# A linear-attention and Fourier-mix kernel on one core: keys and queries transposed on TensorE, 64-row score products, the bonus term through TensorE, and loads in a fixed order

## The chip, the core and the metric

The kernel runs on one core of a Trainium2 chip. A core has five engines, each with its own instruction queue that runs in order: TensorE (PE in the profile; its weight loads are shown apart as PEld), VectorE (DVE), ScalarE (ACT), GpSimd (POOL) and SyncE (SP), which here only issues transfers. Sixteen DMA engines move the data. Matrix products land in PSUM, eight banks of 2 KB for each of 128 partitions; all other tiles lie in SBUF.

The metric is device time in microseconds for one execution. Kernels are compared by the median of their runs.

## The reference

Two stages. The first is a recurrent linear attention: for each batch and head a state of 48 by 48 decays by `w` at each of 768 steps and takes up an outer product; the current step's own product enters the output with the weight `u` in place of the decay. The second adds the real part of a Fourier transform over sequence and model width, normalizes, and runs an MLP of two products with a residual.

```python
# B, H, S, D = 4, 8, 768, 48
for t in range(S):
    cur = np.einsum('bhd,bhe->bhde', u[None] * kt, vt)
    y[:, :, t] = np.einsum('bhd,bhde->bhe', rt, state + cur)
    state = w[None, :, :, None] * state + np.einsum('bhd,bhe->bhde', kt, vt)
...
mixed = np.real(np.fft.fft(np.fft.fft(x, axis=1), axis=2))
u = x + mixed                      # d_model = 384
un = (u - mean(u)) / np.sqrt(var(u) + 1e-06)
out = u + np.maximum(un @ w_ch1, 0.0) @ w_ch2      # 384 -> 1536 -> 384
```

## The kernel before

**Attention.** Each batch (4) is cut into 6 chunks of 128 steps, and each chunk holds all 8 heads. Keys are scaled by a falling power of the decay (`wpn`, L172) and queries by a rising one (`wpp`, L176), both into one bfloat16 tile `KR` of 12 blocks of 128 columns: four blocks with the keys of two heads each (pairs, heads at columns 0 and 64), and eight with the queries of one head each, the other half zero. A DMA transpose (L181) turns the whole tile into `KRT`. Four products (L195) give the scores of the chunk in two PSUM tiles `A_ps`, one with the first four heads, one with the last four; the strictly upper part is kept, for one tile on DVE (L200), for the other by a copy on ACT (L204) and a select on POOL (L205). `y_ps` sums the part of the state (L211, eight products) and the values under the masked scores (L214, eight products). The state is carried by `u_ps` (L219, L222) and scaled by DVE into `Sst` (L224). The bonus term is made apart: POOL multiplies `rt` by `kt` and by `u` (L183, L184), DVE sums over the head (L186), POOL spreads it over the values (L188, `TT`). DVE adds it to `y_ps` (L226): that is `X` of the chunk.

**Fold, Fourier, MLP.** Sums and differences of the two halves of the sequence and of the width (`fold`, L236 to L240) feed the Fourier stage: products with tables (L251), copies by ACT (L253), a reversal by DVE (L256), products with the second tables (L270 to L274), the residual (L276), statistics and normalization (L279 to L289) and a DMA transpose into `UNT` (L291). The MLP of a batch is 2 x (36 + 36) products of 384 columns, L301 and L307, with the ReLU on ACT (L303), the residual on DVE (L310) and the store (L312).

**Order.** The framework puts the instructions of each engine in an order at build time. Attention and Fourier stages have a higher priority than the MLP, and among the former the order of the program counts: attention of batch b+1, then Fourier of b, then the MLP of b-1. All loads, both kinds of DMA transpose, the tables and the stores are issued on SP's queue, where the framework chose their order too; POOL's queue issues the weights. PSUM holds two banks for `A_ps`, one each for `y_ps` and `u_ps`, and four for `mm`, the tile of the Fourier stage and the MLP. Load buffers (`inp`) are five deep, `KR` three, `KRT` three.

Of the kernel before, what the change touches and what calls it, by code (L numbers as in the profile page):

```python
# [62 lines left out]
def kernel(  # L63
# [13 lines left out]
    inp = ctx.enter_context(tc.tile_pool(name="inp", bufs=5))  # L77
# [12 lines left out]
    wall = cp.tile([128, DM + NP], F32, name="wall")  # L90
    nc.vector.memset(wall[:, DM:], 1.0)
    nc.sync.dma_start(out=wall[:, 0:DM], in_=w.rearrange("h d -> (h d)").partition_broadcast(128))
    wv = w.rearrange("(p a) d -> a d p", a=2)
    nc.gpsimd.dma_start(out=wall[0:D, DM:], in_=wv[0])
    nc.gpsimd.dma_start(out=wall[64:64 + D, DM:], in_=wv[1])
# [6 lines left out]
    nc.vector.tensor_scalar(out=ncol, in0=icol, scalar1=-1.0, scalar2=1.0, op0=AluOp.mult, op1=AluOp.subtract)  # L102
    eps_t = cp.tile([128, 1], F32, name="eps_t")
    nc.vector.memset(eps_t, 1e-6)

    lw = cp.tile([128, DM + NP], F32, name="lw")
    nc.scalar.activation(lw, wall, Act.Ln)
    wpp = cp.tile([128, H, D], F32, name="wpp")
    wpn = cp.tile([128, H, D], F32, name="wpn")
    lwr = lw[:, 0:DM].rearrange("p (h d) -> p h d", h=H)  # L110
    nc.scalar.activation(wpn, lwr, Act.Exp, scale=ncol[:, 0:1])  # L111
    nc.scalar.activation(wpp, lwr, Act.Exp, scale=icol[:, 0:1])
    wdec = cp.tile([128, NP], F32, name="wdec")
    nc.scalar.activation(wdec, lw[:, DM:], Act.Exp, scale=float(L))
    WD = cp.tile([128, NP, 2, D], F32, name="WD")
    urow = cp.tile([128, H, D], F32, name="urow")
    ident = cp.tile([128, 128], BF16, name="ident")
    mtri = cp.tile([128, 128], BF16, name="mtri")
# [8 lines left out]
    nc.gpsimd.memset(WD, 0.0)  # L127
    for a in range(2):
        rows = slice(a * 64, a * 64 + 64)
        nc.vector.tensor_copy(WD[rows, :, a, :], wdec[rows, :].unsqueeze(2).to_broadcast([64, NP, D]))  # L130

# [7 lines left out]
    def load_tables():  # L139
        nc.sync.dma_start(out=te_t, in_=te_c.ap())  # L140
        nc.sync.dma_start(out=to_t, in_=to_c.ap())
        nc.sync.dma_start(out=hid_t, in_=hid_c.ap())
        for dt in range(3):
            nc.gpsimd.dma_start(out=W1[:, dt, :], in_=w1[dt * 128:(dt + 1) * 128, :])
        for fg in range(3):
            nc.gpsimd.dma_start(out=W2[:, fg * 4:(fg + 1) * 4, :],
                                in_=w2[fg * 512:(fg + 1) * 512, :].rearrange("(f p) d -> p f d", p=128))

    count = [0]

    def attention(b):
# [4 lines left out]
        for q in range(NQ):  # L156
            i = count[0]
            count[0] += 1
            sl = slice(q * 128, (q + 1) * 128)
            rt = inp.tile([128, H, D], F32, name="rt")  # L160
            kt = inp.tile([128, H, D], F32, name="kt")
            vt = inp.tile([128, H, D], F32, name="vt")
            nc.sync.dma_start(out=kt, in_=k[b, :, sl, :].rearrange("h p d -> p h d"))
            nc.sync.dma_start(out=rt, in_=r[b, :, sl, :].rearrange("h p d -> p h d"))
            nc.sync.dma_start(out=vt, in_=v[b, :, sl, :].rearrange("h p d -> p h d"))
            if i == 0:
                nc.sync.dma_start(out=urow, in_=u.partition_broadcast(128))
                nc.sync.dma_start(out=mtri, in_=mtri_c.ap())
                nc.sync.dma_start(out=ident, in_=id_c.ap())
            KR = KRs[i % NB]  # L170
            K = KR[:, 0:4, :]
            nc.vector.tensor_tensor(out=K.rearrange("t p (a d) -> t p a d", a=2)[:, :, :, 0:D],  # L172
                                    in0=kt.rearrange("t (p a) d -> t p a d", a=2),
                                    in1=wpn.rearrange("t (p a) d -> t p a d", a=2), op=AluOp.mult)
            for a in range(2):
                nc.vector.tensor_tensor(out=KR[:, 4 + a:12:2, a * 64:a * 64 + D], in0=rt[:, a::2, :],  # L176
                                        in1=wpp[:, a::2, :], op=AluOp.mult)
            V = wp.tile([128, H, D], BF16, name="V")
            nc.scalar.copy(V, vt)  # L179
            KRT = wp.tile([128, 12, 128], BF16, name="KRT")  # L180
            nc.sync.dma_start_transpose(out=KRT, in_=KR.rearrange("t c d -> t (c d)"))  # L181
            T1 = wp.tile([128, H, D], F32, name="T1", bufs=2)
            nc.gpsimd.tensor_tensor(out=T1, in0=rt, in1=kt, op=AluOp.mult)  # L183
# [3 lines left out]
            TT = wp.tile([128, H, D], BF16, name="TT")  # L187
            nc.gpsimd.tensor_tensor(out=TT, in0=V, in1=DE.unsqueeze(2).to_broadcast([128, H, D]), op=AluOp.mult)  # L188

# [166 lines left out]
```

## Time and profile before

| | us |
|---|---|
| median of 3 runs | 293.69 (292.69 to 295.96) |
| the profiled execution | 292.54 |
| its span in the trace | 290.8 |
| DMA transposes `KRT`, issue to landing | 24 of 4.1 (median) |
| loads k, r, v, issue to landing | 72 of 3.6 to 3.7 (median) |
| `te_t` needed / landed | PE waited 9.3 |

In the profile's groups a row gives line, engine, operation, tiles with partitions by elements, count, busy us in all, mean ns of one, and the idle time ahead of it with what ended it. Busy time of PE counts a product from its start to its modelled end, and products overlap in the array; so what a stream of products costs is read from the distance between starts, not from the mean of one. A group with more than one shape has a mean of them all.

### The profile page before, as it was taken

How to read it: one execution, taken by the hardware profiler on the slowest of the kernel's cores; microseconds unless marked ns; L12 is line 12 of the kernel's file. 1: busy time of each engine (PE TensorE's matmuls, PEld its weight loads, DVE VectorE, ACT ScalarE, POOL GpSimd, SP SyncE). 2: the span in 40 equal slices, each digit the busy share in tenths (PEclk: the TensorE clock that was granted, in tenths of full speed). 3: DMA queues.
4: the chain of work that ended last, by engine and by line, in shares of the span. 5: the costliest groups of instructions: out<-in, count | busy, mean ns of one | idle time of the engine just before them, and what ended most of it. 6: DMA issues, size and time to landing. Idle time of an engine off the chain costs nothing. (4 is left out here: it accounts for less than half of the span.)

```text
span 290.8 us, 3776 instructions
## 1 busy us (share of the span) xinstructions
PE 178.5 (61%) x1336; PEld 110.2 (38%) x1336; DVE 152.2 (52%) x318; ACT 105.5 (36%) x208; POOL 97.5 (34%) x113
## 2 busy tenths in 40 slices
PE   0034123011643264098654697999699996999995
PEld 0023112001432142055532364656355564666662
DVE  0494459816977589339799885519210290201202
ACT  2701110020221122046232396742928429256170
POOL 8665452978488725002766522000000000000000
PEclk9999999999999999999955799999899999999999
DMA  6899999999988999910962409310501104201102
GB/s 141 169 193 179 200 196 187 188 218 211 193 172 160 175 199 205 246 62 0 189 111 54 95 12 206 98 55 0 112 27 54 57 0 108 83 11 70 56 27 81
DMA packets 128546, 34.91 MB, mean 120 GB/s; under 512 B 122896, under 2 KB 127760, under 8 KB 128528
## 3 DMA queue, kind: packets, MB, share of 16 engines
q1 hardware_dynamic: 126448, 32.32, 53.8%
q0 software_dynamic: 2080, 2.36, 5.4%
q8 instruction: 10, 0.16, 0.2%
q14 instruction: 8, 0.07, 0.1%
HBM read 20.52 MB, written 4.72 MB: 87 GB/s over the span
## 5 line engine op out<-in xcount | busy, mean ns | idle before, releaser
L303 ACT ACTIVATE HT<-mm 128x384 bf16<-128x384 f32 x96 | 44.9, 489 | 28.4 <-PE mm L301 28.3
L301 PE MATMUL mm<-UNT,W 128*128 128x384 bf16 x288 | 51.9, 337 | 4.9 <-ACT HT L303 4.6
L307 PE MATMUL mm<-W,HT 128*128 128x384 bf16 x288 | 50.0, 326 | 0.0
L310 DVE TENSOR_TENSOR osb<-mm,UF 128x384 f32<-128x384 f32 x24 | 13.3, 555 | 68.6 <-PE mm L307 68.4
L195 PE MATMUL A_ps<-KRT 128*128 128x256 bf16 x96 | 22.7, 381 | 30.9 <-DMA KRT<-KR 28.6
L301 PEld LDWEIGHTS <-W 128*128 128x128 bf16 x288 | 28.7, 100 | 25.5 <-issue 8.3
L204 ACT CAST AC<-A_ps 128x512 bf16<-128x512 f32 x24 | 14.0, 585 | 60.4 <-PE A_ps L195 60.4
L307 PEld LDWEIGHTS <-HT 128*128 128x128 bf16 x288 | 27.8, 98 | 17.5
L188 POOL TENSOR_TENSOR TT<-V,DE 128x384 bf16<-128x384 bf16 x24 | 20.0, 836 | 42.8 <-DVE X L226 26.2
L219 PE MATMUL u_ps<-V,KR 128*128 128x96 bf16 x80 | 9.5, 257 | 39.7 <-ACT V L179 18.4
L183 POOL TENSOR_TENSOR T<-rt,kt 128x384 f32<-128x384 f32 x24 | 25.9, 1078 | 12.3 <-DMA rt<-in_r_dram 9.4
L179 ACT CAST V<-vt 128x384 bf16<-128x384 f32 x24 | 12.3, 512 | 47.5 <-DMA vt<-in_v_dram 26.0
L176 DVE TENSOR_TENSOR KR<-rt,wpp 128x192 bf16<-128x192 f32 x48 | 26.0, 573 | 3.5 <-DMA rt<-in_r_dram 3.2
L172 DVE TENSOR_TENSOR KR<-kt,wpn 128x384 bf16<-128x384 f32 x24 | 18.7, 784 | 15.6 <-ACT wpn L111 9.8
L184 POOL TENSOR_TENSOR T<-T,urow 128x384 f32<-128x384 f32 x24 | 26.4, 1104 | 1.3
L205 POOL TENSOR_SCALAR_AFFINE_SELECT MA<-AC 128x512 bf16<-128x512 bf16 x24 | 16.8, 702 | 26.0 <-ACT AC L204 21.1
L195 PEld LDWEIGHTS <-KRT 128*128 128x128 bf16 x96 | 10.4, 125 | 38.3 <-DMA KRT<-KR 33.8
L219 PEld LDWEIGHTS <-KR 128*128 128x128 bf16 x80 | 6.6, 121 | 43.0 <-issue 17.8
L214 PE MATMUL y_ps<-V,MA 128*128 128x48 bf16 x192 | 12.4, 205 | 15.6 <-DVE MA L200 9.2
L253 ACT CAST TT<-mm 128x386 bf16<-128x386 f32 (+1 forms) x24 | 12.4, 594 | 22.5 <-PE mm L251 22.5
L200 DVE TENSOR_TENSOR MA<-A_ps,mtri 128x512 bf16<-128x512 f32 x24 | 16.4, 682 | 7.6 <-PE A_ps L195 6.3
L186 DVE TENSOR_REDUCE DE<-T 128x8 f32<-128x384 f32 x24 | 13.1, 545 | 12.0 <-POOL TT L188 10.2
(58 smaller groups left out, 228.4 us busy)
## 6 DMA issues: line engine op xcount, KB each, us to landing
kt<-in_k_dram SPq DMA_DIRECT2D x24, 192.0 KB, 3.6
rt<-in_r_dram SPq DMA_DIRECT2D x24, 192.0 KB, 3.6
vt<-in_v_dram SPq DMA_DIRECT2D x24, 192.0 KB, 3.7
out_dram<-osb SPq DMA_DIRECT2D x24, 192.0 KB, 1.9
W<-in_moe_w_ch_dram POOLq DMA_DIRECT2D x6, 384.0 KB, 7.0
hid_t<-hid_c SPq DMA_DIRECT2D x1, 576.0 KB, 5.2
KRT<-KR SPq DMA_TRANSPOSE x24, 4.1
te_t<-te_c SPq DMA_DIRECT2D x1, 289.5 KB, 4.5
```

The lines of the kernel that those rows point to most:

```text
L172: nc.vector.tensor_tensor(out=K.rearrange("t p (a d) -> t p a d", a=2)[:, :, :, 0:D], in0=kt.rearrange("t (p a) d -> t p a d", a=2), in1=w ...
L176: nc.vector.tensor_tensor(out=KR[:, 4 + a:12:2, a * 64:a * 64 + D], in0=rt[:, a::2, :], in1=wpp[:, a::2, :], op=AluOp.mult)
L183: nc.gpsimd.tensor_tensor(out=T1, in0=rt, in1=kt, op=AluOp.mult)
L184: nc.gpsimd.tensor_tensor(out=T1, in0=T1, in1=urow, op=AluOp.mult)
L188: nc.gpsimd.tensor_tensor(out=TT, in0=V, in1=DE.unsqueeze(2).to_broadcast([128, H, D]), op=AluOp.mult)
L195: nc.tensor.matmul(A_ps[:, 2 * pp:2 * pp + 2, :], lhsT=KRT[:, p, :], rhs=KRT[:, 4 + 2 * p:6 + 2 * p, :], start=(pp == 0), stop=(pp == 1), ...
L200: nc.vector.tensor_tensor(out=MA, in0=A_ps, in1=mtri.unsqueeze(1).to_broadcast([128, 4, 128]), op=AluOp.mult)
L205: nc.gpsimd.affine_select(out=MA, in_=AC, pattern=[[0, 4], [1, 128]], base=0, channel_multiplier=-1, compare_op=AluOp.is_gt, fill=0.0)
L219: nc.tensor.matmul(u_ps[:, p, :, :], lhsT=KR[:, p, :], rhs=V[:, 2 * p:2 * p + 2, :], start=(p == 0), stop=(q == 0 and p == NP - 1), skip_g ...
L301: nc.tensor.matmul(hp, lhsT=W1[:, dt, ft * 128:(ft + 1) * 128], rhs=UNT[:, :, dt, :], start=(dt == 0), stop=(dt == 2))
L303: nc.scalar.activation(out=HT[:, ft, :], in_=hp, func=Act.Relu)
L307: nc.tensor.matmul(op, lhsT=HT[:, ft, j * 128:(j + 1) * 128], rhs=W2[:, ft, :], start=(ft == 0), stop=(ft == 11))
```

## The change

- Keys and queries are loaded into one tile `kr` and scaled by one DVE product (L191) with one table `wtab`; `KR` has 2 x 4 blocks, keys and queries both as pairs of heads, with no half zero.
- The DMA transpose goes. PE transposes the eight blocks through the identity into one PSUM bank `tp` (L202), and ACT copies it to `KRT` (L204).
- The scores are eight products of 128 columns that use 64 rows each (one head, L212): even heads in one `A_ps`, odd heads in the other. The state's part is four products of 96 columns (L233) where there were eight of 48.
- The bonus: DVE multiplies transposed keys by transposed queries (`PR`, L206), four products of 2 columns with the weights `UW` (L229) sum it into eight further columns of the output's PSUM tile (`yd_ps`), ACT copies them (`DE`, L236). Two POOL products and DVE's reduction go.
- One bank moves from `mm` (four to three) to `tp`. `MA` has six buffers, `inp` six. DVE clears `KR` and `WD` in place of POOL.
- Loads: all of a batch are issued in program order on SP (`keep_in_program_order`), batch 0's first, then the tables, then batch 1's; batch b+2's behind the `UNT` transposes of b. Weights are issued by POOL after the third chunk's `TT`. Stores move from SP to POOL.
- Fourier of b now stands ahead of attention of b+1 in the program.
- ACT loads its function tables at two fixed places at the start.

```diff
-    inp = ctx.enter_context(tc.tile_pool(name="inp", bufs=5))
+    inp = ctx.enter_context(tc.tile_pool(name="inp", bufs=6))
...
+    nc.scalar.preload_act_table_set("natural_log_exp_and_others")
...
+    tc.keep_in_program_order(nc.scalar.preload_act_table_set("sqrt_and_others"))
...
-        t = cp.tile([128, 12, 128], BF16, name=f"KR{i}")
-        nc.gpsimd.memset(t, 0.0)
+        t = cp.tile([128, 2, NP, 128], BF16, name=f"KR{i}")
+        nc.vector.memset(t, 0.0)
...
+    def load_weights():
+        with tc.issue_after(marks["tt2"].ins):
+            for dt in range(3):
+                nc.gpsimd.dma_start(out=W1[:, dt, :], in_=w1[dt * 128:(dt + 1) * 128, :])
...
+    def loads(b):
+        ins = []
+        for q in range(NQ):
...
+            sp(nc.sync.dma_start(out=kr[:, 0], in_=k[b, :, sl, :].rearrange("h p d -> p h d")))
+            sp(nc.sync.dma_start(out=kr[:, 1], in_=r[b, :, sl, :].rearrange("h p d -> p h d")))
...
-            KRT = wp.tile([128, 12, 128], BF16, name="KRT")
-            nc.sync.dma_start_transpose(out=KRT, in_=KR.rearrange("t c d -> t (c d)"))
-            T1 = wp.tile([128, H, D], F32, name="T1", bufs=2)
-            nc.gpsimd.tensor_tensor(out=T1, in0=rt, in1=kt, op=AluOp.mult)
-            nc.gpsimd.tensor_tensor(out=T1, in0=T1, in1=urow, op=AluOp.mult)
-            DE = wp.tile([128, H], F32, name="DE")
-            nc.vector.reduce_sum(out=DE, in_=T1, axis=AX.X)
...
+            tp = ps.tile([128, 2, NP, 128], BF16, name="tp", bufs=1)
+            for s in range(2):
+                for p in range(NP):
+                    nc.tensor.transpose(tp[:, s, p, :], KR[:, s, p, :], ident)
+            KRT = wp.tile([128, 2, NP, 128], BF16, name="KRT")
+            nc.scalar.copy(KRT, tp)
+            PR = wp.tile([128, NP, 128], BF16, name="PR")
+            nc.vector.tensor_tensor(out=PR, in0=KRT[:, 0], in1=KRT[:, 1], op=AluOp.mult)
...
+                for a in range(2):
+                    rows = slice(a * 64, a * 64 + 64)
+                    nc.tensor.matmul(A_ps[a][:, p, :], lhsT=KRT[rows, 0, p, :], rhs=KRT[rows, 1, p, :],
+                                     start=(p == 0), stop=(p == NP - 1), skip_group_check=True)
...
+            for p in range(NP):
+                nc.tensor.matmul(yd_ps[:, DM + 2 * p:DM + 2 * p + 2], lhsT=PR[:, p, :], rhs=UW[:, p, :],
+                                 start=(p == 0), stop=False, skip_group_check=True)
...
+                for p in range(NP):
+                    nc.tensor.matmul(y_ps[:, 2 * p:2 * p + 2, :], lhsT=KRT[:, 1, p, :], rhs=Sst[:, p, :, :],
+                                     start=False, stop=False, skip_group_check=True)
+            DE = wp.tile([128, H], F32, name="DE")
+            nc.scalar.copy(DE, yd_ps[:, DM:])
...
-                fp = ps.tile([128, 2, m], F32, name="mm", bufs=4)
+                fp = ps.tile([128, 2, m], F32, name="mm", bufs=3)
...
-            nc.sync.dma_start(out=out[b, row:row + 128, :], in_=osb)
+            nc.gpsimd.dma_start(out=out[b, row:row + 128, :], in_=osb)
...
+    ins = loads(0)
     load_tables()
-    xs = [attention(0)]
+    xs = [attention(0, ins)]
+    load_weights()
+    ins = loads(1)
...
-            if b + 1 < B:
-                xs.append(attention(b + 1))
             if b < B:
                 hs.append(fourier(b, *xs[b]))
+            if b + 1 < B:
+                xs.append(attention(b + 1, ins))
+            if b + 2 < B:
+                ins = loads(b + 2)
```

What this does to the order on three engines follows; a number behind a tile's name tells one buffer in time from another.

SP's queue before, in the loads of batch 1 (`kt`, `rt`, `vt`), with transposes of earlier chunks among them:

```order
L163 DMA kt_985<-in_k_dram 128x8x48
L164 DMA rt_984<-in_r_dram 128x8x48
L163 DMA kt_1043<-in_k_dram 128x8x48
L165 DMA vt_986<-in_v_dram 128x8x48
L164 DMA rt_1042<-in_r_dram 128x8x48
L181 DMA_TRANSPOSE KRT_588<-KR2_99 128x12x128
L165 DMA vt_1044<-in_v_dram 128x8x48
```

SP's queue after, from the last loads of batch 1 to the first of batch 2 (`kr` takes keys and queries):

```order
L171 DMA kr_559<-in_k_dram 128x8x48
L172 DMA kr_559<-in_r_dram 128x8x48
L175 DMA vt_560<-in_v_dram 128x8x48
L320 DMA_TRANSPOSE UNT_600<-UN_640 128x9x128
L320 DMA_TRANSPOSE UNT_646<-UN_686 128x9x128
L171 DMA kr_1057<-in_k_dram 128x8x48
L172 DMA kr_1057<-in_r_dram 128x8x48
```

The transposes of a chunk are gone from the queue, and the only ones left, those of a batch's normalized rows, stand between two batches' loads.

DVE's queue before, in batch 0 (`T1` is the bonus before its sum):

```order
L224 TENSOR_TENSOR Sst_335<-u_ps_329,WD_91 128x384
L172 TENSOR_TENSOR KR1_97<-kt_343,wpn_86 128x8x48
L186 TENSOR_REDUCE DE_296<-T1_293 128x8
L176 TENSOR_TENSOR KR1_97<-rt_342,wpp_85 128x4x48 x2
L186 TENSOR_REDUCE DE_358<-T1_355 128x8
L200 TENSOR_TENSOR MA_303<-A_ps_300,mtri_94 128x512
L226 TENSOR_TENSOR X_109<-y_ps_312,TT_298 128x384
```

DVE's queue after, in batch 1 on the way to batch 2, whose first product `KR0_102` is already there:

```order
L255 TENSOR_TENSOR X_691<-yd_ps_907,TT_918 128x384
L191 TENSOR_TENSOR KR0_102<-kr_1057,wtab_92 128x16x48
L206 TENSOR_TENSOR PR_951<-KRT_949 128x512
L218 TENSOR_TENSOR MA_963<-A_ps_953,mtri_74 128x512
L253 TENSOR_TENSOR Sst_1271<-u_ps_1266,WD_100 128x384
L206 TENSOR_TENSOR PR_1013<-KRT_1011 128x512
L255 TENSOR_TENSOR X_691<-yd_ps_969,TT_980 128x384
```

Three scaling products and a reduction became one scaling product and `PR`; chunks overlap in the order, here with `PR` of one chunk ahead of `X` of the one before.

ACT's queue before, in batch 0:

```order
L204 CAST AC_193<-A_ps_189 128x512
L204 CAST AC_251<-A_ps_247 128x512
L179 CAST V_289<-vt_282 128x384
L204 CAST AC_309<-A_ps_305 128x512
L179 CAST V_351<-vt_344 128x384
```

ACT's queue after, at the same place:

```order
L204 COPY KRT_350<-tp_341 128x1024
L222 CAST AC_367<-A_ps_355 128x512
L196 CAST V_405<-vt_142 128x384
L204 COPY KRT_416<-tp_407 128x1024
L236 COPY DE_379<-yd_ps_370 128x8
L222 CAST AC_433<-A_ps_421 128x512
```

The copy of the transposed tile of the next chunk (`KRT_416`) now stands ahead of the bonus copy of this one (`DE_379`) on the same engine. On PE the order sets, in many chunks, one score product of the next chunk ahead of the eight products of this chunk's masked scores with the values, and the other seven behind. The MLP of batch 0 stands behind Fourier 1: 61 of its products ahead of batch 3's first transposes, most others among batch 3's chunks, and the last few inside Fourier 2.

More of the change, by code (lines that the diff above doesn't have):

```diff
@@ L206, in attention @@
                                             channel_multiplier=-1, compare_op=AluOp.is_gt, fill=0.0)
                 MAs.append(MA)
[L208 to L215 removed]
+            yd_ps = ps.tile([128, DM + H], F32, name="yd_ps", bufs=1)
@@ L304, in mlp @@
         for j in range(3):
-            op = ps.tile([128, DM], F32, name="mm", bufs=4)
+            op = ps.tile([128, DM], F32, name="mm", bufs=3)
             for ft in range(12):
```

151 lines of the change are left out of this document (76 added, 75 removed).

## The prediction

> **What bounds the kernel now.** I read the page first: the span, the busy shares and the forty slices, in which one digit is a tenth of a slice of 7.3 us.
>
> ```profile
> span 290.8 us, 3776 instructions
> PE 178.5 (61%) x1336; PEld 110.2 (38%) x1336; DVE 152.2 (52%) x318; ACT 105.5 (36%) x208; POOL 97.5 (34%) x113
> ...
> PE   0034123011643264098654697999699996999995
> ...
> DMA  6899999999988999910962409310501104201102
> ```
>
> There are two halves. Up to about 125 us the DMA engines are full and PE is nearly idle; from about 180 us PE is full and the DMA engines are not. Next I asked for single lines (minimum, median and maximum in ns, then first and last start) to find the border between the halves.
>
> ```profile
> L226 DVE TENSOR_TENSOR X<-y_ps,TT x24: 527/554/559, 23.0 to 181.6; 128x384 bf16<-128x384 f32 x24
> L301 PE MATMUL mm<-UNT,W x288: 322/326/524, 165.3 to 281.2; 128*128 128x384 bf16 x144
> ```
>
> X (L226) ends a chunk of the attention. The first ends at 23.5 us, the last at 182.2, and the MLP (L301) starts only at 165.3, since it follows the attention of later batches in the order. So the time is that of the last X plus a tail. The tail by stage, with busy us and count for PE, PEld, DVE, ACT and POOL, then clock, DMA share and GB/s; the last row is a dense piece of the attention:
>
> ```profile
> 182.20:203.70 21.50, 21.46 (x143) 13.28 (x142) 11.44 (x30) 10.03 (x21) 0.00 (x0) 1.00 0.18 51
> 203.70:238.70 35.00, 32.70 (x201) 19.32 (x199) 11.06 (x33) 18.27 (x39) 0.00 (x0) 0.95 0.19 52
> 238.70:290.80 52.10, 46.34 (x283) 27.46 (x281) 8.15 (x18) 25.60 (x55) 0.00 (x0) 0.99 0.20 61
> 135.70:163.60 27.90, 15.85 (x174) 10.50 (x174) 24.62 (x48) 9.02 (x17) 18.47 (x20) 0.76 0.64 109
> ```
>
> The first three rows end with the last transforms of batch 2, of batch 3, and the program. Before 182 us the list of waits (total us, times, longest) names the cause:
>
> ```profile
> PEld L195 <- DMA KRT<-KR: 33.8, 16, 7.0
> PE mm L251 <- DMA te_t<-te_c: 9.3, 1, 9.3
> ...
> SPq L181 <- DVE KR L176: 29.5, 9, 9.5
> ```
>
> PE waits for the DMA transposes, and the queue that issues them (SPq L181) itself stands still for 29.5 us until DVE has made their input, with loads queued behind. The Fourier stage even waits for its tables.
>
> **The change, part by part.** I price a chunk of 128 steps on each engine, then the path.
>
> ```profile
> L172 DVE TENSOR_TENSOR KR<-kt,wpn x24: 541/674/1342, 11.2 to 173.8; 128x384 bf16<-128x384 f32 x24
> L172 DVE TENSOR_TENSOR KR<-kt,wpn 128x384 bf16<-128x384 f32 x24 | 18.7, 784 | 15.6 <-ACT wpn L111 9.8 <-DMA KRT<-KR 4.6 <-DMA kt<-in_k_dram 0.9
> L176 DVE TENSOR_TENSOR KR<-rt,wpp x48: 343/351/1664, 13.5 to 175.0; 128x192 bf16<-128x192 f32 x48
> L236 DVE TENSOR_TENSOR EO<-X x6: 348/554/1546, 45.0 to 182.5; 128x384 bf16<-128x384 bf16 x3, 128x1152 bf16<-128x1152 bf16 x3
> 182.50 0.75 DVE L236 TENSOR_TENSOR EO<-X 128x1152 bf16<-128x1152 bf16 x1
> L200 DVE TENSOR_TENSOR MA<-A_ps,mtri 128x512 bf16<-128x512 f32 x24 | 16.4, 682 | 7.6 <-PE A_ps L195 6.3 <-POOL MA L205 1.1 <-issue 0.2
> L224 DVE TENSOR_TENSOR Sst<-u_ps,WD 128x384 bf16<-128x384 f32 x20 | 11.0, 550 | 2.1 <-PE u_ps L222 1.4 <-PE u_ps L219 0.6
> L188 POOL TENSOR_TENSOR TT<-V,DE x24: 817/827/942, 16.1 to 175.9; 128x384 bf16<-128x384 bf16 x24
> L205 POOL TENSOR_SCALAR_AFFINE_SELECT MA<-AC x24: 627/636/951, 21.9 to 180.5; 128x512 bf16<-128x512 bf16 x24
> L204 ACT CAST AC<-A_ps 128x512 bf16<-128x512 f32 x24 | 14.0, 585 | 60.4 <-PE A_ps L195 60.4
> L303 ACT ACTIVATE HT<-mm 128x384 bf16<-128x384 f32 x96 | 44.9, 489 | 28.4 <-PE mm L301 28.3
> L179 ACT CAST V<-vt 128x384 bf16<-128x384 f32 x24 | 12.3, 512 | 47.5 <-DMA vt<-in_v_dram 26.0 <-PE y_ps L214 21.5
> L114 ACT ACTIVATE wdec<-lw 128x4 f32<-128x4 f32 x1 | 0.2, 188 | 0.0
> ```
>
> DVE: L172 at its fastest takes 0.54 us for 384 columns, L176 0.34 for 192, so about 1.04 ns a column, and the merged product of 768 columns takes 0.95. PR is new: in bf16, 384 columns take 0.35 and 1152 take 0.75, so 512 take 0.42. MA 0.68, Sst 0.55 and X 0.55 stay; the reduction goes. Sum 3.15 us a chunk. How much DVE loses beside POOL is open: L172 reaches 1.34 where POOL works. The ends are 0 and all of POOL's remaining 0.64 + 0.83 = 1.46; I take 0.5, because L172's mean of 0.78 is 0.24 above its fastest and two such operations remain. That makes 3.65.
>
> ACT: V 0.51, the new copy of 1024 columns 0.97 (0.585 for 512, and 0.75 ns a column by the step from L303 to L204; twice L204, 1.17, is the other end), AC 0.585, DE 0.19 as L114. Sum 2.26. POOL keeps two operations of four, 1.46.
>
> ```profile
> 20.15 1.03 PE L195 MATMUL A_ps<-KRT 128*128 128x256 bf16 x4 [1.64 <-DMA KRT<-KR]
> 21.54 0.34 PE L214 MATMUL y_ps<-V,MA 128*128 128x48 bf16 x4
> 15.51 0.50 PE L219 MATMUL u_ps<-V,KR 128*128 128x96 bf16 x4 [2.60 <-DVE Sst L224]
> 246.40 5.85 PE mm L307 x36
> ```
>
> PE: four products of 256 columns take 1.03 us, of which about 0.2 is the last one's way out, so a step of 0.105 for 128 columns. L214 steps by 0.043 for 48 columns, L219 by about 0.08 for 96. Eight transposes 0.84, eight score products 0.84 (0.42 if two halves of the rows run at once), bonus 0.18, state 0.30 (half as many products as before), values 0.34, update with identity 0.62. Sum 3.12 at this slow pace and about half at the pace of the tail. The score products come to the same 1024 columns as before, so the transposes are the addition.
>
> DVE is therefore the fullest engine of a chunk. In the dense piece above it was busy 24.62 of 27.90 us (88%). So a chunk costs 3.65 / 0.88 = **4.15 us**, instead of (182.2 - 23.5) / 23 = 6.9 before, where that holds the Fourier stages too.
>
> The transposes that leave the DMA engines leave 72 loads there. Tables, loads and start:
>
> ```profile
> 20.00:40.00 20.00, 6.36 (x60) 4.22 (x60) 10.93 (x18) 2.27 (x4) 11.09 (x14) 1.00 1.23 196
> 10.00 0.99 POOL L183 TENSOR_TENSOR T<-rt,kt 128x384 f32<-128x384 f32 x1 [1.81 <-DMA rt<-in_r_dram]
> rt<-in_r_dram SPq DMA_DIRECT2D x24, 192.0 KB, 3.6
> out_dram<-osb SPq DMA_DIRECT2D x24, 192.0 KB, 1.9
> wall<-in_w_dram POOLq DMA_DIRECT2D x2, 0.8 KB, 4.0
> ```
>
> A load of 0.197 MB at 196 GB/s is 1.0 us, so a chunk's three take 3.0, below 4.15. The 36 of two batches, the tables (1.2 MB) and the weights (2.4 MB written, 4.7 read) are 10.7 to 13.0 MB, done by some 55 to 66 us; batch 1 ends at 72 in the sum below. The weights now go out between POOL's operations after the third TT, six issues that the first MLP does not need before about 109 us: nothing. One table load of ACT falls away at the start and one ahead of the first rstd: inside the figures below.
>
> Start: the second r landed at 10.0 us; DVE's order puts the second and third KR ahead of the first MA, so the third r, at about 13.0 after three more loads, holds it: KR 1.0, MA 0.7, y 0.6, X 0.55 with handovers, the first X ends at 16.0 (before 23.5). If only the chain of chunk 0 counted, it would be 13.5.
>
> ```profile
> 123.50 2.98 PE L251 MATMUL mm<-te_t,XF 128*128 128x386 bf16 x9 [9.32 <-DMA te_t<-te_c]
> ...
> 135.14 0.56 DVE L276 TENSOR_TENSOR UF<-mm,X 128x384 f32<-128x384 f32 x1 [0.63 <-PE mm L274]
> 184.63 0.75 DVE L240 TENSOR_TENSOR XF<-EO 128x1152 bf16<-128x1152 bf16 x1
> ```
>
> A Fourier stage with its input there lasts 12.2 us (123.5 to 135.7); with one chunk woven in I take 13. One mm buffer less could hold PE, but DVE's UF sets that pace, so it costs nothing. A fold takes 3.2 (182.2 to 185.4). By the new order the path is:
> first X 16.0; five chunks 20.75; last fold piece 1.4; Fourier 0 with chunk (1,0) 13; five chunks 20.75; fold 1 3.0 and five chunks 20.75; Fourier 1 with chunk (2,5) 13; 61 MLP products placed ahead of batch 3, at 5.85 / 36 = 0.1625 each, 9.9; six chunks of batch 3 24.9 and 2.0 to fill them (their PE work at the fast pace, 6 x 1.6, and 71 MLP products, 11.5, lie beside). The last X ends at **145.5** instead of 182.2. Then fold and Fourier 2 15.4 (before 21.5, with 36 MLP products in it that are now done), 35.0, 52.1, and 1.0 because the last output goes out on POOL's queue (ends 0.3 and 2.1: the landing of `out_dram` is 1.9, of POOL's small transfer 4.0). The span is 249.0. The profiled execution took 292.54 us for 290.8, so 1.7 is added, and another 1.0 because it lay 1.15 us under the median of 293.69: **252 us**.
>
> The queue of SP now has an order by hand. The transpose of batch 1's UN stands ahead of all loads of batch 3, and UN comes at the end of Fourier 1, near 112 us. The loads of chunk (3,0) then land some 5 us later (3.6 and the issues before it), near 117; PE reaches it near 118: tight, and free only while the MLP lead covers it. The output's move to POOL puts three issues between the masks of batch 3, under 2.1 us, behind MLP products that are already done.
>
> **The rivals.** *The engines need no slack (faster).* DVE at 3.15 with no loss beside POOL, and the Fourier stages take only DVE's 9.3 us: 252 - 21 x 1.0 - 7.4 = 224. For it: less POOL work. Against it: no long piece before shows DVE over 88%. Chance 0.12.
>
> *PE drains between row sizes.* The order sets one 64-row score product of the next chunk ahead of the values of this one and seven behind: up to four changes of row size a chunk. If each waits for the array to empty, about 0.2 us by the way out of L214 (0.34 - 3 x 0.043), PE needs 3.12 + 0.8 = 3.92 a chunk, at 88% 4.45, and 21 chunks cost 6.3 more: 258. Nothing before runs fewer than 128 rows, so the trace is silent. Chance 0.10. The Trainium skill, "TensorEngine Tiling (Array Packing)", section Tiling Modes, says that a change of the tiling mode, not only of the tile, drains TensorE; no run here shows it so far, and by it the sum would be the 258 instead of 252.
>
> *Loads stand behind UNT.* If batches 2 and 3 wait for UN with all 18 loads, 18 us each: 252 + 36 = 288. Against it: batch 2's follow Fourier 0 by some 20 us of other chunks. Chance 0.04.
>
> *The chunk becomes a serial chain (slower).* tp, yd_ps and u_ps have one buffer. KR 0.95, transposes 1.05, copy 0.97, scores 1.05, AC 0.59, mask 0.64, values 0.55, X 0.55 and some handovers make 6.7 us; 21 x 2.55 more gives 306. It decides from 4.15 + (293.7 - 252) / 21 = 6.1 us a chunk. Against it: KR has three buffers, A and the next transposes stand ahead of the values in the order, and tp's own loop is only 2.0. Chance 0.04.
>
> **How the numbers follow.** The forecast has 0.70. Its ends come from the chunk: 3.15 gives 231, and POOL's whole 1.46 gives (3.15 + 1.46) / 0.88 = 5.24 and 275. The range 231 to 269 leaves out most of the fast case, the two slow ones and little else. About 1% is what a measurement here can tell. Faster by over 1% are the forecast, the fast case, the drains and most of the loads: 0.95; same 0.02 and slower 0.03 share the rest.
>
> **What would show it.** The first X near 16 us and the last near 145; chunks of batch 1 and 2 about 4.15 apart with DVE near 88%; the tail from the last X 103.5 us. KR at 0.95 and the copy at 0.97 in their groups. The forecast is wrong if the PE waits name DVE KR behind DMA kr in batch 3, if PE's score products leave gaps of 0.2 us at each change of rows, or if the wait for tp or yd_ps leads the list.

## The result and the profile after

The changed kernel takes **245.01 us** (median of 4 runs, 243.59 to 246.94), beside 293.55 for the kernel before in the same session: a ratio of 0.834, with a 95% interval of 0.8253 to 0.8426. The forecast of 252 us and its range of 231 to 269 hold it. The profiled execution took 246.25 us for a span of 244.5. A time given below is the median of all executions of a run, while its ratio leaves out executions over 1.5% above the fastest of the same kernel, so the two can differ by up to 1%.

The page of the kernel after, first its span and busy shares, then the forty slices of PE and of the DMA engines (a slice is 6.1 us):

```profile
span 244.5 us, 4268 instructions
PE 192.5 (79%) x1640; PEld 122.4 (50%) x1640; DVE 131.8 (54%) x278; ACT 128.5 (53%) x255; POOL 59.8 (24%) x87
...
PE   0369760892869579987889899879999699999991
...
DMA  6999999998699900005999200051010322020101
```

PE now starts in earnest at 12 us, has one hole near 40 us (the seventh digit, 0), and the DMA engines are full up to about 85 us instead of 125. Single lines of the kernel after, with minimum, median and maximum in ns and first and last start:

```profile
L255 DVE TENSOR_TENSOR X<-yd_ps,TT x24: 525/556/558, 16.5 to 143.9; 128x384 bf16<-128x384 f32 x24
L330 PE MATMUL mm<-UNT,W x288: 322/326/337, 105.7 to 233.1; 128*128 128x384 bf16 x144
```

The first X (L255) ends at 17.1 us, the last at 144.5, and the MLP (L330) starts at 105.7 instead of 165.3. The stretches of the kernel after, in the columns used before; the third to fifth are the tail:

```profile
56.00:82.00 26.00, 17.55 (x214) 13.58 (x215) 22.01 (x42) 17.18 (x32) 9.27 (x12) 0.63 1.01 153
82.00:98.90 16.90, 13.45 (x156) 9.87 (x154) 14.06 (x22) 8.03 (x16) 7.53 (x8) 0.55 0.18 32
...
144.50:157.00 12.50, 11.09 (x75) 6.57 (x73) 10.20 (x27) 4.82 (x9) 0.54 (x1) 1.00 0.09 33
157.00:191.00 34.00, 31.56 (x199) 18.79 (x198) 11.01 (x32) 18.54 (x39) 3.24 (x6) 1.00 0.19 53
191.00:244.50 53.50, 46.73 (x285) 27.67 (x283) 8.03 (x17) 25.25 (x54) 7.03 (x13) 0.99 0.19 60
```

The waits of the kernel after (total us, times, longest) no longer have the DMA transposes in them:

```profile
PE tp L202 <- DVE KR L191: 21.5, 7, 8.8
ACT V L196 <- DMA vt<-in_v_dram: 17.9, 5, 10.7
DVE KR L191 <- DMA kr<-in_r_dram: 16.1, 5, 7.8
```

PE waits for KR, and DVE waits to make it until r is loaded. The longest of these waits is the hole near 40 us. The timeline of the kernel after, all engines (start, duration):

```profile
22.68 1.17 POOL L154 DMA_DIRECT2D W<-in_moe_w_ch_dram  x2
...
23.86 3.33 SPq L172 DMA_DIRECT2D kr<-in_r_dram  x1
...
27.29 7.27 SPq L175 DMA_DIRECT2D vt<-in_v_dram  x1
...
43.00 0.96 DVE L191 TENSOR_TENSOR KR<-kr,wtab 128x768 bf16<-128x768 f32 x1 [7.84 <-DMA kr<-in_r_dram]
...
44.54 0.35 DVE L269 TENSOR_TENSOR XF<-EO 128x384 bf16<-128x384 bf16 x1
```

The r of chunk (1,0) is issued at 23.86, just behind the first two of six weight transfers that POOL issues from 22.68 to 31.0 us. KR(1,0) starts 19.1 us after that issue; SP's own issues stretch to 3.33 and 7.27 us. The last piece of batch 0's fold (XF, L269) stands behind KR(1,0) in DVE's queue, so Fourier 0 waits with it, though its last chunk of X was there at 34.8 us.

### The profile page after: what moved, and what is told of

It reads as the page before. It is cut to its first block, busy times and chain, and to the rows that moved or that the text cites. A ratio compares the mean times of both kernels' runs of the same rounds, so it can differ in the third digit from the quotient of the medians.

```text
span 244.5 us, 4268 instructions
## 1 busy us (share of the span) xinstructions
PE 192.5 (79%) x1640; PEld 122.4 (50%) x1640; DVE 131.8 (54%) x278; ACT 128.5 (53%) x255; POOL 59.8 (24%) x87
## 4 chain that ended last, share of the span: by engine, by line
issue 39%; PE 18%; DMA 11%; DVE 11%; POOL 8%; ACT 7%; SPq 4%; POOLq 0%; ACTq 0%; DVEq 0%
DMA kr<-in_r_dram 11%; POOL out_dram L341 4%; PE tp L202 4%; DVE KR L191 3%; PE A_ps L212 3%; POOL TT L238 3%; PE mm L280 2%; DVE PR L206 2%; ACT KRT L204 2%; ACT UN L318 1%; ACT HT L332 1%; PE u_ps L248 1%; POOL MA L223 1%; DVE MA L218 1%; PE mm L330 1%
## 5 line engine op out<-in xcount | busy, mean ns | idle before, releaser
L330 PE MATMUL mm<-UNT,W 128*128 128x384 bf16 x288 | 52.3, 326 | 7.3 <-ACT HT L332 5.3
L336 PE MATMUL mm<-W,HT 128*128 128x384 bf16 x288 | 51.6, 326 | 0.0
L330 PEld LDWEIGHTS <-W 128*128 128x128 bf16 x288 | 27.5, 98 | 26.1 <-issue 9.5
L202 PE MATMUL tp<-ident,KR 128*128 128x128 bf16 x192 | 22.6, 280 | 21.5 <-DVE KR L191 21.5
L341 POOL DMA_DIRECT2D out_dram<-osb x24 | 13.1, 548 | 100.1 <-DVE osb L339 100.1
L336 PEld LDWEIGHTS <-HT 128*128 128x128 bf16 x288 | 27.7, 98 | 16.9
L191 DVE TENSOR_TENSOR KR<-kr,wtab 128x768 bf16<-128x768 f32 x24 | 26.4, 1099 | 16.1 <-DMA kr<-in_r_dram 16.1
L202 PEld LDWEIGHTS <-KR 128*128 128x128 bf16 x192 | 16.4, 127 | 26.5 <-DVE KR L191 25.5
L204 ACT COPY KRT<-tp 128x1024 bf16<-128x1024 bf16 x24 | 24.3, 1012 | 9.9 <-PE tp L202 9.7
L196 ACT CAST V<-vt 128x384 bf16<-128x384 f32 x24 | 12.2, 511 | 18.5 <-DMA vt<-in_v_dram 17.9
L212 PE MATMUL A_ps<-KRT 64*128 64x128 bf16 x192 | 15.5, 270 | 4.5 <-ACT KRT L204 4.1
L255 DVE TENSOR_TENSOR X<-yd_ps,TT 128x384 bf16<-128x384 f32 x24 | 13.2, 550 | 9.5 <-POOL TT L238 8.1
L318 ACT ACTIVATE UN<-UF,nm,rstd 128x384 bf16<-128x384 f32 x24 | 15.2, 701 | 1.9 <-DVE nm L314 1.9
L212 PEld LDWEIGHTS <-KRT 64*128 64x128 bf16 x192 | 8.4, 113 | 12.0 <-ACT KRT L204 9.4
L243 PE MATMUL yd_ps<-V,MA 128*128 128x48 bf16 x192 | 11.3, 202 | 3.6 <-POOL MA L223 1.2
```

The source lines that it names most:

```text
L191: nc.vector.tensor_tensor(out=KR.rearrange("t s p (a d) -> t (s p) a d", a=2)[:, :, :, 0:D], in0=kr.rearrange("t s (p a) d -> t (s p) a d" ...
L202: nc.tensor.transpose(tp[:, s, p, :], KR[:, s, p, :], ident)
L204: nc.scalar.copy(KRT, tp)
L212: nc.tensor.matmul(A_ps[a][:, p, :], lhsT=KRT[rows, 0, p, :], rhs=KRT[rows, 1, p, :], start=(p == 0), stop=(p == NP - 1), skip_group_check ...
L318: nc.scalar.activation(out=UN[:, j, :], in_=UF[:, j, :], func=Act.Identity, scale=rstd[:, j:j + 1], bias=nm[:, j:j + 1])
L330: nc.tensor.matmul(hp, lhsT=W1[:, dt, ft * 128:(ft + 1) * 128], rhs=UNT[:, :, dt, :], start=(dt == 0), stop=(dt == 2))
```

## Experiments

The first question was which part of the change makes the gain: the arithmetic (transposes and bonus on TensorE, halved rows) or the order. The second was what the early weights cost. All ratios are to the kernel before; the kernel after stands at 0.834.

### The order alone, and the arithmetic alone

The kernel before with the order of the kernel after (cut; `UNT` has five buffers here instead of six):

```diff
+    def load_weights():
+        with tc.issue_after(marks["tt2"].ins):
...
+            sp(nc.sync.dma_start(out=kt, in_=k[b, :, sl, :].rearrange("h p d -> p h d")))
...
-            nc.sync.dma_start(out=out[b, row:row + 128, :], in_=osb)
+            nc.gpsimd.dma_start(out=out[b, row:row + 128, :], in_=osb)
...
-    xs = [attention(0)]
+    ins = loads(0)
+    load_tables()
+    xs = [attention(0, ins)]
```

> The arithmetic of the kernel before (twelve blocks of queries and keys turned by DMA, bonus by products on POOL and a sum on DVE, whole-row score products) in the order of the kernel after (loads pinned ahead, tables early, weights from the middle of batch 0, each Fourier stage ahead of the next attention, outputs on POOL's queue). Theory 'the order is the gain': most of the 48.5 us stays, 255 to 265 us, with the MLP starting near 115 us instead of 165. Rival 'the arithmetic is the gain, and the order pays only with it': 278 us or more, since the transposes of batch 0 stand behind all its loads on SP's queue and twelve blocks keep the DMA engines full longer. In between (266 to 277) both count.

Measured: 269.51 us, ratio 0.9055 (0.8936 to 0.9173), between the two ranges; the first MLP product starts at 122.5 us.

The kernel after with the order of the kernel before (cut):

```diff
-        with tc.issue_after(marks["tt2"].ins):
...
-        return tc.keep_in_program_order(ins)
+        return ins
...
-            nc.gpsimd.dma_start(out=out[b, row:row + 128, :], in_=osb)
+            nc.sync.dma_start(out=out[b, row:row + 128, :], in_=osb)
...
+            if b + 1 < B:
+                xs.append(attention(b + 1, loads(b + 1)))
```

> The arithmetic of the kernel after (transposes on TensorE, compact pairs, bonus on TensorE) in the order of the kernel before: no load pinned, tables after the first attention, the next attention placed ahead of the Fourier stage, weights free, outputs on SP's queue. Theory 'the order is the gain': 275 us or more, the MLP starts after 150 us and the first Fourier stage after 100. Rival 'the arithmetic is the gain': within 8 us of the kernel after, 245 to 253. In between both count.

Measured: 269.46 us, ratio 0.9149 (0.9071 to 0.9227). This too lies between the ranges, so neither theory holds alone. The two ratios multiply to 0.828, within the interval of the whole change: **each half gives some 8 to 9%, and each gives it with or without the other.** What the order alone does not cure is the queue of SP. In the waits of the run with the order alone, the transposes still stand for DVE:

```profile
SPq L195 <- DVE KR L190: 36.2, 17, 5.4
```

### The transposes taken back to the DMA engines

```diff
-            tp = ps.tile([128, 2, NP, 128], BF16, name="tp", bufs=1)
-            for s in range(2):
-                for p in range(NP):
-                    nc.tensor.transpose(tp[:, s, p, :], KR[:, s, p, :], ident)
...
-            nc.scalar.copy(KRT, tp)
+            nc.sync.dma_start_transpose(out=KRT.rearrange("t s p c -> t (s p) c"),
+                                        in_=KR.rearrange("t s p c -> t (s p c)"))
```

> The chunk's transposes go back to the DMA engines, with the compact pairs, and the copy by ACT goes; loads stay in their fixed order. On SP's queue the six transposes of batch 0 then stand behind all its loads and the tables, which costs up to 20 us at the start by itself. Theory 1 (the transposes on PE are what makes the gain): above 275 us, with the chunks of batches 1 and 2 above 4.5 us apart. Rival (the order of loads and stages makes it): chunks as far apart as with PE (3.3 to 4), 265 us or less, all of it from the start.

Measured: 257.11 us, ratio 0.8739 (0.8686 to 0.8791), so 12 us are given back of the 48.5, far less than the first theory asks for. The transposes of batch 0 stand behind all its loads on SP's queue. X (here L252) and the wait of PE's weight loads in this run:

```profile
L252 DVE TENSOR_TENSOR X<-yd_ps,TT x24: 526/557/558, 32.2 to 172.0; 128x384 bf16<-128x384 f32 x24
```

```profile
PEld L209 <- DMA KRT<-KR: 23.9, 8, 12.6
```

The first X comes 15.6 us later than in the kernel after, the last 28, so the loss is not all from the start, as the rival had it. The end comes only 10 us later (span 254.8). The time is therefore **not the last X plus a fixed tail**: work that stands behind the last X in the kernel after fills the gaps of the late chunks here. By the last X, 167 of the 576 MLP products (L330 and L336 in the kernel after) have run instead of 127, and the whole of Fourier 2 on PE (from 152.4 to 162 us) lies ahead of it.

### The bonus taken back to POOL and DVE

```diff
-            PR = wp.tile([128, NP, 128], BF16, name="PR")
-            nc.vector.tensor_tensor(out=PR, in0=KRT[:, 0], in1=KRT[:, 1], op=AluOp.mult)
+            T1 = wp.tile([128, H, D], F32, name="T1", bufs=2)
+            nc.gpsimd.tensor_tensor(out=T1, in0=kr[:, 1], in1=kr[:, 0], op=AluOp.mult)
+            nc.gpsimd.tensor_tensor(out=T1, in0=T1, in1=urow, op=AluOp.mult)
+            DE = wp.tile([128, H], F32, name="DE")
+            nc.vector.reduce_sum(out=DE, in_=T1, axis=AX.X)
...
```

> The kernel after with the bonus term as before: two float32 products on POOL (about 1 us and 0.9 us a chunk), a sum of 0.4 us on DVE, no PR, no bonus products on TensorE, no copy of DE. Theory 'POOL and DVE beside each other set the pace of a chunk': POOL comes to 3.4 us a chunk and DVE to 3.6 with contention, a chunk costs about 1 us more in 18 chunks that lie on the path, 255 to 265 us. Rival 'the loads and the handovers set the pace, the engines have slack': 242 to 248 us.

Measured: 262.45 us, ratio 0.8898 (0.8831 to 0.8965), 16 to 17 us given back of the 48.5. The groups of this run (KR is L187, X is L249), and then of the kernel after:

```profile
L187 DVE TENSOR_TENSOR KR<-kr,wtab 128x768 bf16<-128x768 f32 x24 | 31.5, 1314 | 11.0 <-DMA kr<-in_r_dram 11.0
L202 POOL TENSOR_TENSOR T<-kr 128x384 f32<-128x384 f32 x24 | 29.1, 1213 | 25.9 <-DMA kr<-in_r_dram 25.9
...
L249 DVE TENSOR_TENSOR X<-yd_ps,TT 128x384 bf16<-128x384 f32 x24 | 13.3, 555 | 12.8 <-PE yd_ps L237 12.5
```

```profile
L191 DVE TENSOR_TENSOR KR<-kr,wtab 128x768 bf16<-128x768 f32 x24 | 26.4, 1099 | 16.1 <-DMA kr<-in_r_dram 16.1
L204 ACT COPY KRT<-tp 128x1024 bf16<-128x1024 bf16 x24 | 24.3, 1012 | 9.9 <-PE tp L202 9.7
...
L206 DVE TENSOR_TENSOR PR<-KRT 128x512 bf16<-128x512 bf16 x24 | 12.9, 537 | 1.0 <-ACT KRT L204 1.0
```

With two more products on POOL, KR takes 1.31 us in the mean instead of 1.10, while X, which reads one operand from PSUM, stays at 0.555. The Trainium skill, "GPSIMD Engine Reference", section Specifications, says that POOL's way to SBUF is shared with VectorE, and that VectorE's instructions with two operands in SBUF contend for it; the trace agrees in these two groups. In the page's chain of the work that ended last, first of this run and then of the kernel after, POOL grows to the largest engine:

```profile
issue 39%; POOL 30%; DVE 12%; PE 8%; ACT 4%; DMA 3%; SPq 2%; POOLq 1%; DVEq 0%
```

```profile
issue 39%; PE 18%; DMA 11%; DVE 11%; POOL 8%; ACT 7%; SPq 4%; POOLq 0%; ACTq 0%; DVEq 0%
```

So the old bonus lengthens the path through POOL, as the theory has it. How much of the 16 to 17 us is slower DVE products, and how much POOL's own two products and their handovers, this run does not part.

### Whole rows in the score products

Each score product contracts both heads of its pair over 128 rows, for the number and width of products as after; the scores are then sums over two heads.

```diff
-                    nc.tensor.matmul(A_ps[a][:, p, :], lhsT=KRT[rows, 0, p, :], rhs=KRT[rows, 1, p, :],
+                    nc.tensor.matmul(A_ps[a][:, p, :], lhsT=KRT[:, 0, p, :], rhs=KRT[:, 1, p, :],
```

> The eight score products use all 128 rows, that is both heads of a pair at once, so the scores and the output are not those of the reference; their number and columns stay. Theory (PE does not set the pace): within 1.5 us of 245, though a burst of eight takes 0.9 to 1.05 us instead of 0.61 and the 0.14 us at each change of rows go. Rival (PE sets the pace and row packing is part of the gain): 3 to 8 us slower; if the changes of rows cost more than the packing brings, 2 to 6 us faster.

Measured: 245.18 us, ratio 0.8328 (0.826 to 0.8396): the same as after. A change of rows in PE's timeline, of the kernel after and then of this run:

```profile
29.95 0.29 PE L212 MATMUL A_ps<-KRT 64*128 64x128 bf16 x1 [0.68 <-ACT KRT L204]
30.17 0.50 PE L243 MATMUL yd_ps<-V,MA 128*128 128x48 bf16 x8
```

```profile
29.26 0.23 PE L212 MATMUL A_ps<-KRT 128*128 128x128 bf16 x1 [0.83 <-ACT KRT L204]
29.33 0.36 PE L243 MATMUL yd_ps<-V,MA 128*128 128x48 bf16 x8
```

Between a 64-row product and the next of 128 rows the starts lie 0.22 us apart, without the change of rows 0.07. PE's pace is lower in the first pair (0.29 beside 0.23 for one product); a step of its transposes is 0.10 at that pace, so a change costs some 0.12 us, an estimate from these rows. The drain that the Trainium skill names in "TensorEngine Tiling (Array Packing)", Tiling Modes, is there, but small. The run takes away two things at once: the changes of rows, and the gain of 64 rows (eight score products take 0.62 us here and 0.40 in the kernel after, both at the higher pace). That the time stays shows that the two together do not reach the end; that each alone is free is not shown.

### Where the weights are issued

The first trial puts the weights behind the third chunk of batch 1 instead of the third of batch 0:

```diff
-        with tc.issue_after(marks["tt2"].ins):
+        with tc.issue_after(marks["tt8"].ins):
...
+            if b == 0:
+                load_weights()
```

> The weights of the MLP are issued by POOL after the third TT of batch 1 instead of batch 0; nothing else moves. Theory 1 (the weights share the DMA engines with the loads of batch 1 and stretch the first of them from 4 to 19 us to landing): r of chunk (1,0) lands within 6 us of its issue, DVE no longer idles 7.8 us ahead of KR, the Fourier stage 0 starts 6 to 8 us earlier, median 236 to 240 us. Rival (the DMA engines are full with loads and tables alone, so the wait only moves): 243 us or more.

Measured: 246.67 us, ratio 0.8367 (0.8304 to 0.843): no gain. KR(1,0) starts at 34.7 instead of 43.0, but the wait moves to the loads behind the weights, which is KR(2,1) here. DVE's wait in this run:

```profile
DVE KR L191 <- DMA kr<-in_r_dram: 17.5, 5, 9.0
```

The second trial issues them behind the first chunk of batch 2, for the DMA engines of the kernel after are empty from about 85 us:

```diff
-        with tc.issue_after(marks["tt2"].ins):
+        with tc.issue_after(marks["tt12"].ins):
...
+            if b == 1:
+                load_weights()
```

> The weights are issued after the bonus product of the first chunk of batch 2 instead of the third of batch 0, where the DMA engines fall idle. Theory 'the weights cost the wait of 7.8 us for r of chunk (1,0), because the DMA engines are full until batch 2 is loaded': that wait falls below 2 us and no later load waits longer than 3 us, time 234 to 241 us. Rival 'the wait is not on the path any more, since PE catches up at its full clock in the MLP stage': the waits go, the time stays at 243 to 247 us. If the weights come too late for the first MLP the first HT waits for W and the time is above 247.

Measured: **238.23 us**, ratio 0.8074 (0.8001 to 0.8146), below the interval of the kernel after. KR(1,0) in DVE's timeline, without a wait ahead of it, the wait in the list, and the MLP in the lines of this run:

```profile
34.58 0.95 DVE L191 TENSOR_TENSOR KR<-kr,wtab 128x768 bf16<-128x768 f32 x1
```

```profile
DVE KR L191 <- DMA kr<-in_r_dram: 8.6, 4, 3.7
```

```profile
L330 PE MATMUL mm<-UNT,W x288: 322/326/337, 96.7 to 225.9; 128*128 128x384 bf16 x144
```

Of the waits that are left, 7.0 of 8.6 us lie ahead of the first three KR, at the start. KR(1,0) comes 8.4 us earlier, the MLP 9.0, the end 7.1 (span 237.4). The early weights thus cost about 7 us. The forecast had priced their issue at nothing.

### The order in its parts

The transposes of UN left free on SP's queue:

```diff
-            sp(nc.sync.dma_start_transpose(out=UNT.rearrange("p j c t -> p (j c) t"),
-                                           in_=UN.rearrange("p j d -> p (j d)")))
+            nc.sync.dma_start_transpose(out=UNT.rearrange("p j c t -> p (j c) t"),
+                                        in_=UN.rearrange("p j d -> p (j d)"))
```

> Only the transposes of UN are no longer held in the program's order on SP, so one of batch 1's two stands later among the loads of batch 3. Theory (the loads of batch 3 land late because both stand ahead): KR of chunk (3,0) starts 2 to 3 us earlier, 242 to 244 us. Rival (what PE waits for there is covered): within 1 us of 245.

Measured: 246.45 us, ratio 0.8368 (0.8312 to 0.8425). In the trace only batch 0's transposes had moved, with loads of batch 1 now between them, and the loads of batch 3 were still issued at 115 us, so this tells nothing on those loads.

The loads left free among each other:

```diff
-        return tc.keep_in_program_order(ins)
+        return ins
```

> The kernel after with the loads of r, k and v not pinned among each other: for the first two batches nothing changes but a transpose of UN that moves among the loads, for batch 3 the loads of k and r now stand ahead of both transposes of batch 1's UN. Theory 'the loads of batch 3 behind UN cost time': KR of chunk (3,0) starts before 112 instead of 119 us and the time is 239 to 243 us. Rival 'the first products of the MLP cover them, as the forecast had it': 244 to 247 us.

Measured: 259.06 us, ratio 0.8828 (0.877 to 0.8886), which no theory expected. SP's timeline in this run shows why, with ACT's wait behind it:

```profile
72.38 1.98 SPq L171 DMA_DIRECT2D kr<-in_k_dram  x2
74.41 3.20 SPq L172 DMA_DIRECT2D kr<-in_r_dram  x3
78.03 2.67 SPq L175 DMA_DIRECT2D vt<-in_v_dram  x3
```

```profile
ACT V L196 <- DMA vt<-in_v_dram: 23.3, 4, 11.6
```

The scheduler sends k and r of batch 2 first and only then the v that chunk (1,5) still needs: its X slips from 81.3 to 93.3 us. A fixed order of the loads is worth 14 us in this kernel. How much of it is this v is not shown, since the chunks of batch 3 moved as well (KR(3,0) starts at 99 us instead of 119); for the same reason the run says little on the loads of batch 3.

The stages swapped back (attention of the next batch ahead of the Fourier stage), with all else as after:

```diff
-            if b < B:
-                hs.append(fourier(b, *xs[b]))
             if b + 1 < B:
                 xs.append(attention(b + 1, ins))
+            if b < B:
+                hs.append(fourier(b, *xs[b]))
```

> The kernel after with one change of its order: the attention of the next batch is placed ahead of the Fourier stage, as in the kernel before; loads, tables, weights and outputs keep their places in the queues. Theory 'of the order, this placing is the larger part': 258 to 268 us, and the first MLP starts 15 us or more later than 106. Rival 'the loads and tables issued early are the larger part': 245 to 252 us.

Measured: 242.26 us, ratio 0.819 (0.8114 to 0.8267), below both ranges. The interval meets that of the kernel after, so neither a loss nor a gain is shown, and what the rival says stands: the part of the order that pays is not the place of the stages, which leaves the loads, tables and stores. MLP 0 here begins early (its first HT at 85.0 us), just ahead of the chunks of batch 2, whose first KR starts at 88.1.

The transposes of UN on ACT's queue, on top of the late weights (whose lines are left out):

```diff
-            sp(nc.sync.dma_start_transpose(out=UNT.rearrange("p j c t -> p (j c) t"),
+            (nc.scalar.dma_start_transpose(out=UNT.rearrange("p j c t -> p (j c) t"),
```

> The kernel with the weights behind the first chunk of batch 2, and besides the transposes of UN issued from ACT's queue, so that no load on SP's queue stands behind them. With the loads of batch 3 out of UN's way 235 to 237 us, if they are on the path; 238 to 239 as with the late weights alone if the MLP's first products cover them; above 239 if the issues hold up ACT.

Measured: 252.57 us, ratio 0.857 (0.8482 to 0.8659), 14 us slower than the late weights alone. X and the MLP in this run:

```profile
L255 DVE TENSOR_TENSOR X<-yd_ps,TT x24: 529/557/559, 16.4 to 128.6; 128x384 bf16<-128x384 f32 x24
```

```profile
L330 PE MATMUL mm<-UNT,W x288: 322/326/528, 106.7 to 240.8; 128*128 128x384 bf16 x144
```

With its loads early, the first chunks of batch 3 moved ahead of Fourier 1 in the queues (KR(3,0) starts at 88 instead of 110 us). The last X is 7 us earlier than with the late weights alone, but the MLP starts 10 us later, and only 34 of its 576 products have run by the last X instead of 122. How much ACT's issues add to that was not tried.

### Both together

Stages swapped, weights behind the third chunk of batch 1, where that order leaves the DMA engines empty:

```diff
-        with tc.issue_after(marks["tt2"].ins):
+        with tc.issue_after(marks["tt8"].ins):
...
             if b + 1 < B:
                 xs.append(attention(b + 1, ins))
+            if b == 0:
+                load_weights()
+            if b < B:
+                hs.append(fourier(b, *xs[b]))
...
```

> The attention of the next batch ahead of the Fourier stage, and the weights issued behind the third chunk of batch 1, in the stretch in which the DMA engines were empty in the run with the stages swapped alone (about 50 to 80 us there). Theory 'the early weights cost a wait on the path whichever stage comes first': the wait of KR(1,0) for r falls from 8 us to under 1 and the time from 242 to 234 to 237 us, below 238.2. Rival 'with the stages swapped the wait is covered, since chunks of batch 1 catch up in front of Fourier 0': 240 to 244 us.

Measured: **232.53 us** (232.01 to 233.91), ratio 0.7878 (0.7836 to 0.7919), better than either kernel and below the range of its own theory. The lines of its MLP and, from its list of waits, KR:

```profile
L330 PE MATMUL mm<-UNT,W x288: 322/326/337, 78.7 to 220.7; 128*128 128x384 bf16 x144
```

```profile
DVE KR L191 <- DMA kr<-in_r_dram: 7.4, 4, 3.8
```

The wait ahead of KR(1,0), 8.7 us with the stages swapped alone, is gone here too (it starts at 34.7), so it was on the path with either stage first.

## Why the prediction was right, and where it was not

- **The bound of before** was read rightly: the DMA transposes and the queue that issued them. Taking them back costs 12 us, taking the bonus back 16 to 17, undoing the order 24.
- **The path by its steps** shows that the total is nearer than its parts. Times in us, from the end of one step to the end of the next:

| step | said | measured | difference |
|---|---|---|---|
| first X | 16.0 | 17.1 | +1.1 |
| five chunks of batch 0 | 20.8 | 17.7 | -3.1 |
| last fold piece, Fourier 0 with chunk (1,0) | 14.4 | 23.0 | +8.6 |
| ten chunks and fold 1 | 44.5 | 41.1 | -3.4 |
| Fourier 1, to the first MLP product | 13.0 | 6.8 | -6.2 |
| to the last X | 36.8 | 38.8 | +2.0 |
| tail | 103.5 | 100.0 | -3.5 |
| span | 249.0 | 244.5 | -4.5 |

- **The weights at nothing**: the failed step, and the +8.6. It compared their bytes with the end of batch 1 and not with the first chunk of it. By the price of 196 GB/s used there, 18 loads, the tables and k and r of chunk (1,0) are 5.1 MB, or 26 us; 4.7 MB read for the weights are 24 more, or 12 by the 2.4 MB written, so KR(1,0) was to be expected at 38 to 50 us, an estimate, and not by 36.8, where batch 0 was to end. It came at 43.0, after a wait of 7.8, and Fourier 0 with it. The runs give 7 us for this.
- **A Fourier stage** was priced too high, and this cancels most of the failed step. The 12.2 us read in the old trace hold 15 products of the next batch's stage, from 131.78 to 134.62 us:

```profile
131.78 1.19 PE L251 MATMUL mm<-te_t,XF 128*128 128x386 bf16 x6
133.11 0.66 PE L251 MATMUL mm<-te_t,XF 128*128 128x386 bf16 x3
133.65 1.14 PE L251 MATMUL mm<-to_t,XF 128*128 128x384 bf16 x6
```

  In the kernel after, Fourier 1 lasts 9.5 us from its first product to its last UF (98.4 to 107.9). The first MLP product runs at 105.7, before that, where the forecast had put it behind the stage and chunk (2,5).
- **A chunk**: 4.15 us said. The distances between the X of one batch do not measure it, because DVE's order moves KR products of later chunks ahead: five distances of batch 0 (3.54 each) hold three KR, five of batch 1 (4.8) hold seven, four of batch 2 (3.2) hold two. From the first X of batch 1 to the fifth of batch 2 there are ten chunks and ten KR in 41.1 us, or 3.8 a chunk when the fold's 3.0 is taken off. The mis-sized term is the loss beside POOL: 0.27 in the mean (KR 1.10 for 0.95, PR 0.54 for 0.42) and not 0.5, though KR took 1.41 to 1.61 in the full stretch of batch 0. With 0.27 the forecast's own sum gives 3.42 / 0.88 = 3.9. DVE was busy 93% of the stretch from 16.5 to 34.8 us and 84% of those ten chunks, on both sides of the 88% that was said. ACT's new copy took 1.01 for 0.97.
- **Loads of batch 3 behind UN**: "tight" was right. KR(3,0) waited 1.24 us for r and PE 0.74 us for it, so one of the signs of a wrong forecast is there, with a small size. No run isolates this.
- **The tail**: 100.0 us (12.5, 34.0, 53.5). The first term's reason was wrong: Fourier 2's input was ready at 112 us, and what follows the last X at 144.5 is the fold of batch 3. Fourier 2 stands behind batch 3 in PE's order, not for want of its input. What made the tail come out is that the forecast's count of MLP products ahead of the last X, 61 and 71, was near the 127 of the trace. With 167, and Fourier 2 done as well, the tail is 82 us (transposes by DMA); with 34 it is 123 (UN on ACT's queue).
- **The rivals**: drains of PE are real, some 0.12 us a change, and do not show in the time together with the gain of 64 rows. The serial chain did not appear: `tp` waits for KR, not for its one buffer. DVE without slack came close in batch 0 alone (93%).

So the mechanism of the gain was right, and that the span came within 4.5 us is in part luck: a missing wait of 8.6 us met a Fourier stage, a chunk and a tail that were each priced too high.

## What to carry over

Price a transfer that is moved earlier by what lands behind it: the bytes in front of the first chunk that needs a load, not the sum over a stage. In a kernel whose last stage is dense products on PE, count how much of that stage has run when the stage ahead of it ends. Neither the end of the attention nor the start of the MLP gives the time alone: beside the late weights alone, the run with UN on ACT's queue finished the attention 7 us sooner and the program 14 us later, and the run with the stages swapped started the MLP 12 us sooner and ended no sooner. Before you price a stage from an old trace, see whose products lie in it. Where a scheduler may reorder loads, pin them, and then test each neighbour in the queue by itself.

## What the hardware showed beside that

- A transfer's issue can hold its queue: SP's issues of r and v took 3.33 and 7.27 us while the weights were in flight, and 0.58 and 3.22 in the run with the weights behind batch 2.
- PE's granted clock is not one number for a kernel. In the kernel after it is 0.63 and 0.55 from 56 to 99 us, in the rows above. With the stages swapped, chunks of batch 2 and MLP products together fill a stretch of 26 us at the full clock:

```profile
88.00:114.00 26.00, 21.48 (x273) 13.38 (x274) 18.60 (x35) 18.88 (x39) 11.72 (x14) 1.00 1.30 178
```

- Nor does a granted clock of 1.00 give PE's pace. In the kernel after, eight transposes take 1.04 us in the stretch of batch 0 and 0.62 in batch 3, though 1.00 is granted in both; the row of batch 0 and the two groups of transposes:

```profile
16.50:34.80 18.30, 15.47 (x173) 11.02 (x172) 17.07 (x30) 8.75 (x17) 12.12 (x16) 1.00 1.18 218
```

```profile
27.81 1.04 PE L202 MATMUL tp<-ident,KR 128*128 128x128 bf16 x8
120.17 0.62 PE L202 MATMUL tp<-ident,KR 128*128 128x128 bf16 x8 [0.74 <-DVE KR L191]
```

  The cause stays open.
